# A hand-ordered attention and feed-forward kernel: a new order of all calls and loads, turns by DMA or TensorE chosen per tile, word-wide zero fills, and a tail in two unequal pieces

## The chip, the core and the metric

The kernel runs on one core of a Trainium2 chip. A core has five engines with queues of their own, which work side by side and wait for each other by semaphores: PE (TensorE, matrix products from SBUF into PSUM), DVE (VectorE), ACT (ScalarE), POOL (GpSimd) and SP (SyncE, which here only issues DMA transfers). Each engine takes its instructions strictly in the order of the program. The metric is the device time of one launch in microseconds (us).

## The reference

Two parts follow each other. The first is an attention over blocks whose keys and values are mixed across blocks by a matrix that is normalized in Sinkhorn's manner, five times over:

```python
P = sort_net                                   # [4, 8, 8, 8]
for _ in range(5):
    P = P - np.max(P, axis=-1, keepdims=True)
    P = np.exp(P)
    P = P / (np.sum(P, axis=-1, keepdims=True) + 1e-09)
    P = P / (np.sum(P, axis=-2, keepdims=True) + 1e-09)
k_sorted = np.einsum('bhij,bhjcd->bhicd', P, k_b)   # 8 blocks of 96 rows, head size 64
v_sorted = np.einsum('bhij,bhjcd->bhicd', P, v_b)
scores = scale * np.matmul(q_b, k_sb.transpose(0, 1, 2, 4, 3))
attn = softmax(scores)                         # within each block of 96
out = np.matmul(attn, v_sb)                    # [4, 8, 768, 64]
```

The second is a feed-forward part on the 3072 tokens of 512 features, with weights 512 x 2048 and 2048 x 512:

```python
h = x @ w_in
g = h * np.cos(h)
return (g @ w_out).astype(np.float32)          # [3072, 512]
```

## The kernel before

The 3072 tokens are worked in eight tiles of 384 (n = 0 to 7). A tile is half of one batch: four blocks of 96 rows (u = 0 to 3), all eight heads. The whole order of the program is one hand-written list of calls, PLAN; a loop (L722) takes the calls in turn and each emits its instructions. The list so fixes the order on every engine. A bank name in a call (B0, B1, B2: two PSUM banks each; C0, C1: one each) says where TensorE writes, and a call that starts with `e` empties that result with ACT (A) or DVE (V).

What a tile goes through, by call names:

- `qk` scores of one block: 4 matmuls of 192 columns (tile 0: 16 smaller ones). `mx` takes the maximum and subtracts it (DVE, L561 to L577), `ex` is the exponential (ACT, L582).
- The probabilities are turned, either by TensorE (`pp`, 8 transposes into PSUM, and an eviction) or by a DMA transpose issued by SP (`pd`, L592).
- `av` multiplies by the values (8 matmuls), `xn` divides by the sums (DVE, L619 and L621).
- The result is turned into xT, by TensorE (`xp`, 4 transposes and an eviction) or by DMA (`xd`, L630).
- `up` is the first projection, 4 accumulating matmuls per 128 of the 2048 hidden features (L653); `ga` takes the cosine by ACT (L663) and the product by DVE (L670) into `gall`; `dn` is the second projection, 4 matmuls of 512 columns a call, four calls for 128 rows (L678). `oc` copies out of PSUM, `st` stores.

Before the first tile there is the Sinkhorn normalization in two halves (`b_...` calls): short steps that go round ACT, PE and DVE. The mixed keys come from `k0`, `k1` and `kg`, the mixed values from `v0`, `v1` and `vg` (TensorE, then an eviction). Values for the upper positions are first reordered by POOL (`vp`, L487). The keys of a head pair lie in four slots: an eviction fills two of them, SP copies half of each to the other two (`ksw`, L472 and L474), and POOL writes zeros into what is left (`z_k`, L338), two of those fills after the copies have read their source.

Loads are issued by POOL (`ld_...`), because they convert float32 to bfloat16 on the way: q in two whole halves for tiles 0 and 1 (`ld_qr`, turned by TensorE with `q0` and `qp`), then by block (`ld_q`, turned by a DMA transpose, `qd`, L435); k and v for the first two batches (`ld_k`, `ld_v`) and for the other two (`ld_kg`, `ld_vg`); the weights in quarters (`ld_wi`, `ld_wo`). `hold` (L409) is a one-column copy on POOL that makes POOL wait for a given tile before it issues what follows.

`w` calls are idle matmuls on a constant tile (L343), 112 in all: they keep TensorE active where it would wait. The last 128 rows are not done by `dn` but by `tail` (L695): two halves of 256 columns, each with 16 matmuls, in the banks C0 and C1, emptied by ACT, and by DVE and ACT, and stored from SP and ACT.

## Time and profile before

| what | us |
|---|---|
| three runs | 242.86, 253.38, 252.88 |
| their median | 252.88 |
| span of the profiled execution | 242.1 |
| PE busy in it | 234.3 |
| DVE busy | 171.7 |
| ACT busy | 151.4 |
| POOL busy | 82.7 |
| bytes read from HBM, written | 27.27 MB, 6.29 MB |

The profile is of one execution with a span of 242.1 us, close to the lowest of the three runs. Busy time of PE contains the idle matmuls. The views quoted further down are the page of the profile, the windows (busy time of each engine and the granted TensorE clock in a stretch of time), the timeline of one engine (start, duration, instruction, and in brackets what ended its idle time), the chain (the work that ended last, followed back), and the view of one line of the program, which for a DMA gives the time from issue to landing.

### The profile page before, as it was taken

The page shows a single profiled execution, that of the slowest core. Times are in us where ns is not written, and L with a number is a line of the kernel's source. Part 1 is how long each engine was busy: PE and PEld are TensorE (multiplying, and loading weights), DVE is VectorE, ACT ScalarE, POOL GpSimd, SP SyncE. Part 2 cuts the span into 40 slices and gives each one's busy share as a digit, 9 for nine tenths or more (in the row PEclk, how much of TensorE's full clock was granted, in tenths as well). Part 3 has the DMA queues.
Part 4 walks back from the last instruction along what each step waited for, and adds up shares of the span by engine and source line. Part 5 has one row for each costly group of instructions (what it writes and reads, how often), then busy time and mean ns, then how long its engine had stood idle before and what let it go on. Part 6 is the DMA issues. An engine that isn't in the chain of part 4 may idle for free.

```text
span 242.1 us, 5306 instructions
## 1 busy us (share of the span) xinstructions
PE 234.3 (97%) x2166; PEld 152.0 (63%) x2166; DVE 171.7 (71%) x301; ACT 151.4 (63%) x210; POOL 82.7 (34%) x85
## 2 busy tenths in 40 slices
PE   8999999996999999999999999999999999999994
PEld 5867889954676566655666646655565555555553
DVE  5328767994688976898579989799969758616610
ACT  3175768675498777876587935683776479425601
POOL 8867599604981013999532300000000000000000
PEclk9999999997999999999999999999999999999999
DMA  7999996999999988798593974015862570450211
GB/s 88 212 203 195 205 190 79 125 226 154 139 152 216 191 160 171 114 145 116 94 130 73 102 124 105 0 27 115 212 102 49 129 81 2 109 190 0 87 71 62
DMA packets 64232, 29.91 MB, mean 124 GB/s; under 512 B 53584, under 2 KB 59728, under 8 KB 63952
## 3 DMA queue, kind: packets, MB, share of 16 engines
q0 software_dynamic: 26080, 13.63, 42.7%
q1 hardware_dynamic: 37616, 15.74, 29.9%
q8 instruction: 17, 0.28, 0.5%
q10 hardware_dynamic: 512, 0.20, 0.3%
q14 instruction: 7, 0.06, 0.1%
HBM read 27.27 MB, written 6.29 MB: 139 GB/s over the span
## 4 chain that ended last, share of the span: by engine, by line
PE 78%; DMA 10%; POOL 6%; ACT 2%; DVE 1%; issue 1%; DVEq 0%; ACTq 0%; SPq 0%
PE h L653 30%; PE o L678 25%; PE idle L343 7%; DMA pT<-p_buf 5%; DMA w_out_t<-in_moe_w_out_dram 5%; POOL vperm L487 3%; PE av L609 3%; PE sc L531 3%; PE vs L495 2%; PE o L701 1%; PE xps L638 1%; PE vs L513 1%; PE sk L354 1%; POOL q_mem L283 1%; PE pps L599 1%
## 5 line engine op out<-in xcount | busy, mean ns | idle before, releaser
L678 PE MATMUL o<-w_out_t,gall 128*128 128x512 bf16 x368 | 89.5, 382 | 1.9 <-DMA w_out_t<-in_moe_w_out_dram 1.9
L653 PE MATMUL h<-xT,w_in_t 128*128 128x384 bf16 (+1 forms) x576 | 88.6, 308 | 0.0
L670 DVE TENSOR_TENSOR gall<-c,h 128x768 bf16<-128x768 f32 x64 | 60.1, 950 | 22.4 <-ACT c L663 21.7
L663 ACT ACTIVATE c<-h,half_pi 128x768 f32<-128x768 f32 x64 | 57.2, 901 | 22.0 <-PE h L653 21.0
L653 PEld LDWEIGHTS <-w_in_t 128*128 128x128 bf16 x576 | 53.6, 98 | 27.1
L678 PEld LDWEIGHTS <-gall 128*128 128x128 bf16 x368 | 34.3, 99 | 33.8 <-issue 2.7
L582 ACT ACTIVATE p_buf<-s 96x768 bf16<-96x768 f32 x32 | 26.3, 839 | 4.5 <-DVE s L577 3.0
L487 POOL COPY vperm<-kv 128x1536 bf16<-128x1536 bf16 (+1 forms) x10 | 28.2, 2837 | 1.3 <-DMA kv<-in_v_dram 1.3
L568 DVE TENSOR_REDUCE mx<-sc 96x4 f32<-96x384 f32 (+1 forms) x39 | 28.1, 720 | 0.8 <-PE sc L531 0.7
L577 DVE TENSOR_TENSOR s<-sc,mx 96x384 f32<-96x384 f32 (+1 forms) x33 | 24.3, 736 | 2.2
L283 POOL DMA_DIRECT2D q_mem<-in_q_dram x24 | 18.8, 787 | 17.8 <-DMA q_turned<-q_mem 17.0
L621 DVE TENSOR_TENSOR xn<-av,r 96x512 bf16<-96x512 f32 x32 | 22.0, 687 | 1.1
L343 PE MATMUL idle<-warm 128*128 128x256 bf16 x112 | 18.6, 304 | 1.1 <-DVE half_pi L309 1.0
L247 ACT COPY o_s<-o 128x512 f32<-128x512 f32 (+2 forms) x10 | 5.3, 531 | 16.1 <-PE o L678 12.2
L343 PEld LDWEIGHTS <-warm 128*128 128x128 bf16 x112 | 11.2, 112 | 4.2 <-DVE half_pi L309 1.0
L338 POOL MEMSET kPg<- 64x768 bf16 (+1 forms) x8 | 13.6, 1704 | 0.2
L619 DVE RECIPROCAL r<-av 96x8 f32<-96x8 f32 x32 | 6.4, 199 | 9.2 <-PE av L609 9.1
L531 PEld LDWEIGHTS <-q_turned 128*128 128x128 bf16 x112 | 9.8, 99 | 4.3
L247 ACT COPY xT<-xps 128x384 bf16<-128x384 bf16 x11 | 5.3, 478 | 11.2 <-PE xps L638 11.2
L247 ACT COPY kv<-o 128x512 f32<-128x512 f32 x9 | 5.2, 580 | 10.6 <-PE o L678 10.6
L247 ACT CAST vS<-vs 96x512 bf16<-96x512 f32 x15 | 8.5, 585 | 5.0 <-PE vs L495 4.9
L531 PE MATMUL sc<-kPg,q_turned 128*128 128x192 bf16 x80 | 10.9, 246 | 0.0
(106 smaller groups left out, 229.9 us busy)
## 6 DMA issues: line engine op xcount, KB each, us to landing
out_dram<-kv SPq DMA_DIRECT2D x12, 256.0 KB, 2.4
out_dram<-o_s SPq DMA_DIRECT2D x11, 256.0 KB, 2.8
q_mem<-in_q_dram POOLq DMA_DIRECT2D x24, 96.0 KB, 4.7
w_out_t<-in_moe_w_out_dram POOLq DMA_DIRECT2D x4, 512.0 KB, 9.9
w_in_t<-in_moe_w_in_dram POOLq DMA_DIRECT2D x4, 512.0 KB, 18.5
kv<-in_v_dram POOLq DMA_DIRECT2D x2, 768.0 KB, 11.7
kv<-in_k_dram POOLq DMA_DIRECT2D x2, 768.0 KB, 8.5
kv<-in_v_dram POOLq DMA_DIRECT2D x6, 256.0 KB, 9.9
```

The costliest lines, as they stand in the source:

```text
L247: A.copy(dst, src)
L343: nc.tensor.matmul(idle[:], warm[:], warm[:, :1].to_broadcast([128, 256]), start=True, stop=True)
L487: G.tensor_copy(dst, src)
L531: nc.tensor.matmul(out, q_turned[n % 2][:, c:c + 128], keys, start=True, stop=True)
L568: V.reduce_max(m[:], scv, axis=AX.X)
L577: V.tensor_tensor(dst, scv, m.to_broadcast([blk, w, H2, blk]), op=ALU.subtract)
L582: A.activation(p[:, :, :blk], s_t.pop((n, u)).rearrange("p z a c -> p (z a) c"), AF.Exp, scale=scale)
L621: V.tensor_tensor(x[:], avv[:, :, :, :D], r.to_broadcast([blk, 2, H2, D]), op=ALU.mult)
L653: nc.tensor.matmul(hv[f], w_in_t[:, kk, (f0 + f) * 128:(f0 + f + 1) * 128], x_of(n)[:, kk, lo:hi], start=(kk == 0), stop=(kk == KC - 1))
L663: A.activation(cc, hh, AF.Sin, bias=half_pi[:, 0:1])
L670: V.tensor_tensor(dst, cc, hh, op=ALU.mult)
L678: nc.tensor.matmul(out_ps[n, ts][:], gall[:, g_at(n, f), ts * 128:(ts + 1) * 128], w_out_t[:, f, :], start=(f == 0), stop=(f == FC - 1))
```

## The change

All calls stand in a new order, with other banks and other evicting engines. Apart from that order:

- Idle matmuls: 36 instead of 112, and none at the end.
- Turns: tile 2's probabilities go by TensorE (12 `pp` and 20 `pd` calls instead of 8 and 24), and xT goes by DMA more often (18 `xd` and 14 `xp` instead of 12 and 20).
- Three of the four `hold` calls that made POOL wait for turned tiles go or move: `hold p 3 3` and `hold qt 1` go, `hold p 2 3` stands at the end of the list.
- Loads: sort_net first, then q, k, v, q, v, all of w_in, then w_out in the order 3, 0, 2, 1, then the second batch's keys. Before, the first quarter of w_out stood ahead of v and w_in, and the other three behind the second batch's keys.
- `z_k` writes its zeros as 32-bit words. The copy that makes `maskp` is a call of its own.
- `ex` takes a free buffer from a list that `pd` and `pp` fill again.
- `dn` accumulates its four parts in any order; the call that comes first opens the accumulation and the fourth closes it.
- The last tile's results go to memory of their own in the key buffer (`kept` 2). The last 128 rows are done by `dl`, in 384 and 128 columns, in two banks, interleaved with the other rows of the tile; `ol` empties and stores them (DVE and SP, ACT and ACT).

The first and last lines of the new list, and the diff of the functions:

```diff
+    "ld_s", "z_warm", "w 3 B2", "z_id", "z_mask", "w 3 B2", "z_maskp", "b_max 0", "b_max 1", "ld_qr 0",
+    "b_exp0 0", "b_ci 0", "b_exp0 1", "ld_k 0", "b_rows 0", "w 1 C1", "b_turn 0 C0", "b_cols 0", "w 2 B2",
+    "b_ci 0", "w 2 B0", "b_exp 0", "z_same", "b_sum 0 B1", "ld_v 0", "q0 1 B0", "z_tail", "b_inv 0",
+    "b_norm 0", "w 4 C0", "ld_qr 1", "b_ci 1", "b_ci 0", "b_exp 0", "z_pi", "z_k 0 1", "b_sum 0 C0",
+    "z_pad", "ld_v 1", "e q0 1 V", "b_inv 0", "b_norm 0", "q0 3 B2", "b_ci 0", "q0 2 B0", "b_rows 1",
+    "b_exp 0", "q0 0 C0", "b_sum 0 C1", "b_inv 0", "w 1 B1", "e q0 0 A", "z_ones 0", "b_norm 0", "w 3 C0",
+    "ld_wi 2", "ld_wi 3", "b_ci 0", "z_order", "e q0 2 V", "w 1 C0", "b_exp 0", "ld_wi 1", "b_sum 0 C0",
+    "b_inv 0", "b_norm 0", "b_ci 0", "b_turn 1 C1", "w 2 C0", "w 4 C0", "ld_wi 0", "b_end 0", "e q0 3 A",
+    "b_cols 1", "k0 0 0 16 C0", "k0 0 16 16 B2", "k0 0 32 16 B0", "b_ci 1", "e k0 0 0 16 V",
+    "e k0 0 16 16 V", "b_v B1", "k0 1 16 16 C0", "k0 1 32 16 C1", "e k0 0 32 16 A", "e k0 1 32 16 A",
+    "e b_v V", "qk 0 3 2 B0", "v0 2 24 8 B1", "b_exp 1", "e k0 1 16 16 V", "qk 0 0 2 B2", "ld_wo 3",
+    "e v0 2 24 8 A", "v0 2 8 8 C1", "vp 0 32 16", "k0 1 0 16 B1", "e v0 2 8 8 A", "mx 0 3 2",
+    "e k0 1 0 16 A", "ksw 0 1", "v0 2 16 8 B0", "v0 2 32 8 C1", "qk 0 1 2 B1", "w 1 C0", "e v0 2 32 8 A",
+    "w 2 C0", "vp 0 48 16", "b_sum 1 C0", "mx 0 0 2", "e v0 2 16 8 A", "w 1 B2", "ex 0 0 0", "mx 0 1 2",
...
+    "ga 6 12 2 0 384", "up 6 10 2 0 384 B2", "pd 7 0", "av 7 1 B1", "st 4 2 S", "dn 6 0 0 C1", "st 5 2 S",
+    "ex 7 3 1", "pd 7 3", "dn 6 2 1 B0", "st 5 1 S", "hold p 2 3", "xn 7 1", "av 7 0 B1", "st 2 2 S",
+    "xn 7 0", "dn 6 1 3 C0", "ga 6 10 2 0 384", "dn 6 2 0", "dn 6 1 1", "av 7 3 B1", "xd 7 1", "xd 7 0",
+    "xn 7 3", "dn 6 1 0", "xd 7 3", "av 7 2 B2", "dn 6 2 2", "dn 6 0 2", "dn 6 1 2", "xn 7 2", "dn 6 0 1",
+    "xd 7 2", "dn 6 2 3", "oc 6 2 A 1", "up 7 6 2 0 384 B2", "up 7 4 2 0 384 B0", "up 7 10 2 0 384 B1",
+    "oc 6 1 V 1", "ga 7 6 2 0 384", "dn 6 0 3", "ga 7 4 2 0 384", "up 7 2 2 0 384 B2", "dn 7 1 1 C0",
+    "st 6 1 S", "ga 7 10 2 0 384", "up 7 12 2 0 384 B0", "up 7 0 2 0 384 B1", "oc 6 0 A 1", "st 6 0 S",
+    "ga 7 2 2 0 384", "ga 7 12 2 0 384", "up 7 8 2 0 384 B2", "up 7 14 2 0 384 B0", "ga 7 0 2 0 384",
+    "dn 7 0 0 B1", "dn 7 0 1", "dl 0 1 C1", "st 6 2 S", "ga 7 8 2 0 384", "ga 7 14 2 0 384", "dn 7 1 3",
+    "dl 0 2", "dn 7 0 3", "dn 7 1 2", "st 5 0 S", "dn 7 1 0", "oc 7 1 A 2", "dl 0 3", "dn 7 0 2",
+    "oc 7 0 A 2", "dl 0 0", "dl 1 2 B2", "dl 1 3", "dl 1 0", "dl 1 1", "st 7 1 S", "st 7 0 S", "ol 0 V S",
+    "ol 1 A A",
...
@@ -327,6 +328,8 @@
 
     def z_same():
         V.tensor_copy(same, rows_of)
+
+    def z_maskp():
         V.tensor_copy(maskp.rearrange("p (b e x) -> p b e x", b=2, e=2),
                       maskh.rearrange("p (b x e) -> p b e x", b=2, e=2))
 
@@ -335,7 +338,7 @@
     def z_k(g, part):
         t, (rows, s) = KP[g], ((slice(64, 128), 1), (slice(0, 64), 2),
                                (slice(64, 128), 0), (slice(0, 64), 3))[part]
-        G.memset(t[rows, s], 0.0)
+        G.memset(t[rows, s].rearrange("p m t -> p (m t)").bitcast(FP32), 0.0)
 
     def w(times, pool):
         idle = pool[0].tile([128, 256], FP32, name="idle", tag=pool[1])
@@ -518,7 +521,7 @@
 
     ROWS = 2
     s_t, pb, pT, av_t, xn_t, xT, sc_t = {}, {}, {}, {}, {}, {}, {}
-    cnt = [0]
+    free = list(range(NP))
 
     def scores(n, u, h2, out):
         g, b2, ih = where(n)
@@ -577,8 +580,8 @@
             V.tensor_tensor(dst, scv, m.to_broadcast([blk, w, H2, blk]), op=ALU.subtract)
 
     def ex(n, u, late):
-        p = p_bufs[cnt[0] % NP]
-        cnt[0] += 1
+        i = free.pop(0)
+        p = p_bufs[i]
         A.activation(p[:, :, :blk], s_t.pop((n, u)).rearrange("p z a c -> p (z a) c"),
                      AF.Exp, scale=scale)
         if late:
@@ -586,14 +589,18 @@
             t = vperm[:, z * w:(z + 1) * w].rearrange("p (a c) -> p a c", c=blk)
         else:
             t = ptp.tile([128, H, blk], BF16, name="pT", tag="pT")
-        pT[n, u], pb[n, u] = t, p
+        pT[n, u], pb[n, u] = t, i
 
     def pd(n, u):
+        i = pb.pop((n, u))
+        free.append(i)
         nc.sync.dma_start_transpose(
-            out=pT[n, u][:], in_=pb.pop((n, u)).rearrange("p a c -> p (a c)"))
+            out=pT[n, u][:], in_=p_bufs[i].rearrange("p a c -> p (a c)"))
 
     def pp(n, u, pool):
-        p = pb.pop((n, u))
+        i = pb.pop((n, u))
+        free.append(i)
+        p = p_bufs[i]
         ps = pool[0].tile([128, H, 128], BF16, name="pps", tag=pool[1])
         for a in range(H):
             nc.tensor.transpose(ps[:blk, a, :blk], p[:, a, :blk], ident[:blk, :blk])
@@ -602,7 +609,7 @@
     def av(n, u, pool):
         g, b2, ih = where(n)
         a = pool[0].tile([128, 2, 512], FP32, name="av", tag=pool[1])
-        pt = pT.pop((n, u)).rearrange("p a c -> p (a c)")
+        pt = pT[n, u].rearrange("p a c -> p (a c)")
         for e in range(H):
             h2, hp = e // 2, e % 2
             w = 128 if e < H - 1 else blk
@@ -669,56 +676,57 @@
             hh = hh.rearrange("p z (f c) -> p z f c", f=half)
         V.tensor_tensor(dst, cc, hh, op=ALU.mult)
 
-    out_ps, o_sb = {}, {}
-
-    def dn(n, ts, part, pool=None):
-        if part == 0:
-            out_ps[n, ts] = pool[0].tile([128, Dm], FP32, name="o", tag=pool[1])
-        for f in range(part * FC // 4, (part + 1) * FC // 4):
-            nc.tensor.matmul(
-                out_ps[n, ts][:], gall[:, g_at(n, f), ts * 128:(ts + 1) * 128], w_out_t[:, f, :],
-                start=(f == 0), stop=(f == FC - 1))
+    out_ps, o_sb, parts = {}, {}, {}
+
+    LAST = (B * S // TC - 1, TC // 128 - 1)
+    CUT = (slice(0, 3 * Dm // 4), slice(3 * Dm // 4, Dm))
+
+    def dn(n, ts, part, pool=None, z=None):
+        c = slice(0, Dm) if z is None else CUT[z]
+        key = (n, ts, z)
+        if key not in out_ps:
+            out_ps[key] = pool[0].tile([128, c.stop - c.start], FP32, name="o", tag=pool[1])
+            parts[key] = 0
+        parts[key] += 1
+        fs = range(part * FC // 4, (part + 1) * FC // 4)
+        for f in fs:
+            nc.tensor.matmul(
+                out_ps[key][:], gall[:, g_at(n, f), ts * 128:(ts + 1) * 128], w_out_t[:, f, c],
+                start=(parts[key] == 1 and f == fs[0]), stop=(parts[key] == 4 and f == fs[-1]))
 
     def oc(n, ts, eng, kept):
         if kept:
-            z = (n % 2 * 3 + ts) * 2 * Dm
-            o_s = vbuf[:, z:z + 2 * Dm].bitcast(FP32)
+            z = (ts if kept == 2 else n % 2 * 3 + ts) * 2 * Dm
+            o_s = (vbuf, vbuf, kbuf[:, CD // 2:])[kept][:, z:z + 2 * Dm].bitcast(FP32)
         else:
             o_s = op.tile([128, Dm], FP32, name="o_s", tag="o_s")[:]
-        copy_on(eng, o_s, out_ps.pop((n, ts))[:])
+        copy_on(eng, o_s, out_ps.pop((n, ts, None))[:])
         o_sb[n, ts] = o_s
 
     def st(n, ts, queue):
         r0 = n * TC + ts * 128
         queue.dma_start(out=out[r0:r0 + 128, :], in_=o_sb.pop((n, ts)))
 
-    def tail():
-        n, ts, w = 7, TC // 128 - 1, Dm // 2
-        for z in range(2):
-            pool = POOL[("C0", "C1")[z]]
-            o = pool[0].tile([128, w], FP32, name="o", tag=pool[1])
-            for f in range(FC):
-                nc.tensor.matmul(
-                    o[:], gall[:, g_at(n, f), ts * 128:(ts + 1) * 128],
-                    w_out_t[:, f, z * w:(z + 1) * w], start=(f == 0), stop=(f == FC - 1))
-            o_s = op.tile([128, w], FP32, name="o_s", tag="o_s")
-            for e, (eng, dma) in enumerate(
-                    (((A, nc.scalar),), ((V, nc.sync), (A, nc.scalar)))[z]):
-                c = slice(e * w // 2, (e + 1) * w // 2) if z else slice(0, w)
-                copy_on(eng, o_s[:, c], o[:, c])
-                dma.dma_start(
-                    out=out[n * TC + ts * 128:(n + 1) * TC, z * w:(z + 1) * w][:, c],
-                    in_=o_s[:, c])
+    def dl(z, part, pool=None):
+        dn(*LAST, part, pool, z)
+
+    def ol(z, eng, queue):
+        c = CUT[z]
+        r0 = LAST[0] * TC + LAST[1] * 128
+        at = CD // 2 + LAST[1] * 2 * Dm
+        o_s = kbuf[:, at:at + 2 * Dm].bitcast(FP32)[:, c]
+        copy_on(eng, o_s, out_ps.pop((*LAST, z))[:])
+        queue.dma_start(out=out[r0:r0 + 128, c], in_=o_s)
 
     calls = dict(
         ld_s=ld_s, ld_k=ld_k, ld_v=ld_v, ld_kg=ld_kg, ld_vg=ld_vg, ld_qr=ld_qr, ld_q=ld_q,
         ld_wi=ld_wi, ld_wo=ld_wo, z_id=z_id, z_p=z_p, z_ones=z_ones, z_warm=z_warm, z_pi=z_pi,
-        z_pad=z_pad, z_tail=z_tail, z_order=z_order, z_mask=z_mask, z_same=z_same, z_k=z_k, w=w,
+        z_pad=z_pad, z_tail=z_tail, z_order=z_order, z_mask=z_mask, z_same=z_same, z_maskp=z_maskp, z_k=z_k, w=w,
         b_exp0=b_exp0, b_rows=b_rows, b_turn=b_turn, b_cols=b_cols, b_exp=b_exp, b_sum=b_sum,
         b_norm=b_norm, b_inv=b_inv, b_ci=b_ci, b_max=b_max,
         b_end=b_end, b_v=b_v, hold=hold, q0=q0, qp=qp, qd=qd, k0=k0, k1=k1, kg=kg,
         ksw=ksw, vp=vp, v0=v0, v1=v1, vg=vg, qk=qk, mx=mx, ex=ex, pd=pd, pp=pp, av=av, xn=xn, xd=xd,
-        xp=xp, up=up, ga=ga, dn=dn, oc=oc, st=st, tail=tail)
+        xp=xp, up=up, ga=ga, dn=dn, oc=oc, st=st, dl=dl, ol=ol)
     made = {}
     for call in PLAN:
         name, *args = call.split()
@@ -728,7 +736,7 @@
             continue
         key = (name, *(a for a in args if a not in POOL))
         args = [POOL[a] if a in POOL else a for a in args]
-        if name == "st":
+        if name in ("st", "ol"):
             args[2] = QUEUE[args[2]]
         args = [ENG[a] if isinstance(a, str) and a in ENG else a for a in args]
         args = [int(a) if isinstance(a, str) and a.isdigit() else a for a in args]
```

211 rows, old and new, of the table PLAN are left out of this document.

## The prediction

> **What bounds the kernel now.** First the page's busy shares and its chain, and the group of the idle matmuls among the costliest groups.
>
> ```profile
> span 242.1 us, 5306 instructions
> PE 234.3 (97%) x2166; PEld 152.0 (63%) x2166; DVE 171.7 (71%) x301; ACT 151.4 (63%) x210; POOL 82.7 (34%) x85
> ...
> PE 78%; DMA 10%; POOL 6%; ACT 2%; DVE 1%; issue 1%; DVEq 0%; ACTq 0%; SPq 0%
> ...
> L343 PE MATMUL idle<-warm 128*128 128x256 bf16 x112 | 18.6, 304 | 1.1 <-DVE half_pi L309 1.0
> ```
>
> TensorE is the engine of the end: 97% busy, 78% of the chain. But 112 of its 2166 matmuls compute nothing (the program calls them `w`), so busy is not useful here. The second view is the windows, cut where the work changes: Sinkhorn, tile 0's attention, tile 0's up-projections, the place around a wait, and the rest.
>
> ```profile
> core 0: us, PE busy (x) PEld busy (x) DVE busy (x) ACT busy (x) POOL busy (x), PEclk, DMA share, GB/s
> ...
> 14.90:33.80 18.90, 18.47 (x346) 15.29 (x346) 12.44 (x22) 11.27 (x21) 14.75 (x10) 1.00 1.22 204
> 33.80:53.60 19.80, 19.80 (x277) 17.02 (x274) 16.24 (x27) 15.64 (x22) 12.18 (x12) 1.00 1.01 145
> 53.60:61.40 7.80, 5.91 (x46) 3.56 (x43) 3.89 (x10) 4.71 (x8) 3.65 (x4) 0.78 0.99 173
> ...
> 67.50:120.00 52.50, 52.03 (x447) 32.35 (x446) 42.28 (x72) 39.56 (x54) 28.60 (x25) 1.00 0.99 154
> 120.00:170.00 50.00, 49.80 (x383) 29.84 (x381) 43.51 (x67) 33.10 (x41) 6.48 (x10) 1.00 0.55 83
> 170.00:234.00 64.00, 64.00 (x418) 35.74 (x417) 42.09 (x57) 37.23 (x45) 0.00 (x0) 1.00 0.39 90
> ```
>
> From 67.5 to 234 us TensorE pauses 0.47 + 0.20 us in all. No new order can win there; it can only lose. What can be won is the time before the first up-projection, one disturbed place, and the end. TensorE's timeline shows the three.
>
> ```profile
> 1.01 4.88 PE L343 MATMUL idle<-warm 128*128 128x256 bf16 x22 [1.01 <-DVE half_pi L309]
> ...
> 14.87 1.36 PE L446 MATMUL ks<-bd,kv 64*128 64x32 bf16 x48
> ...
> 33.78 1.49 PE L653 MATMUL h<-xT,w_in_t 128*128 128x192 bf16 x16
> ...
> 53.56 1.03 PE L678 MATMUL o<-w_out_t,gall 128*128 128x512 bf16 x4
> 56.48 1.02 PE L678 MATMUL o<-w_out_t,gall 128*128 128x512 bf16 x4 [1.89 <-DMA w_out_t<-in_moe_w_out_dram]
> 57.34 0.28 PE L354 MATMUL sk<-E,kPg 128*128 128x8 f32 x2
> 57.48 1.47 PE L678 MATMUL o<-w_out_t,gall 128*128 128x512 bf16 x4
> ...
> 233.99 1.16 PE L343 MATMUL idle<-warm 128*128 128x256 bf16 x9
> ```
>
> The first up-projection starts at 33.78 us. From there every microsecond of TensorE's stream is useful except the wait before 56.48, its after-effect, and nine idle matmuls at 233.99. So I make the sum as a shift of TensorE's stream: how much earlier or later the same work ends.
>
> **The change part by part.**
>
> *Weights of the down-projection.* The wait at 56.48 ends with the landing of the last quarter of w_out:
>
> ```profile
> 44.77 11.67 DMA w_out_t<-in_moe_w_out_dram
> ```
>
> The matmuls at 53.56 should last 4 x 0.216 = 0.86 us, to 54.42; the next ones start at 56.48, which is 2.06 us lost. After it four matmuls take 1.47 instead of 1.03 us, and the window around it has a clock of 0.78: 0.22 x 7.8 = 1.7 us more. In the new order all four quarters are queued on POOL before the second batch's keys, and the down-projection takes the quarters in the order of the loads (3, 0, 2, 1). Ahead of the last quarter stand two 384 KB halves of q, three 768 KB loads of k and v, and 4 + 4 weight quarters of 512 KB: 7.3 MB. At the 204 GB/s of the second window that is 36 us, so about 38 us. TensorE asks for that quarter after 32.7 us of useful work, which by the old pace is 49 us or later. The wait goes: **-3.7 us**. Late next would be the second batch's keys, 0.8 MB or 4 us behind (42 us), first used near 53 us.
>
> *Nine idle matmuls before the tail.* They lasted 234.99 - 233.99: **-1.0 us**. The two pieces of the last row block (384 and 128 columns) now go to banks of their own, so nothing has to be emptied first, and their 32 matmuls stream the same columns. What lies behind the last matmul I leave at its old length, within 0.3 us: the last piece is smaller, but the 384-column store is larger than any that was last before.
>
> *Turns on TensorE instead of by DMA.* Tile 2's four probability turns (32 transposes) come to TensorE, and six fewer xT turns stay there.
>
> ```profile
> 61.95 0.36 PE pps L599 x8
> ...
> 63.65 0.17 PE xps L638 x4
> ```
>
> 4 x 0.36 - 6 x 0.17 = **+0.4 us** of TensorE work. The four evictions that come with it lie in a stretch where the vector engine is busy 42.3 of 52.5 us. The removed DMA turns take some of the 0.67 us of later pauses with them: **-0.4 us**.
>
> *The way to the first up-projection.* Three things change: the zero fills leave the start, 36 idle matmuls stand where 112 stood, and more useful work is pulled ahead of the first up-projection: both q turns of tile 1 (2 x 0.46 us), eight v1 matmuls, two score parts, one xT turn and two Sinkhorn sums, together 2.0 us at the pitches of the same calls in TensorE's timeline. What sets the moment is not TensorE but the vector engine behind the scores:
>
> ```profile
> 13.84 0.35 DVE L392 SCALAR_TENSOR_TENSOR bd<-maskp,ci,T 128x128 bf16<-128x128 f32 x1
> ...
> 18.37 0.95 DVE L561 TENSOR_REDUCE mx<-sc 96x8 f32<-96x768 f32 x1 [3.92 <-PE sc L542]
> 19.36 0.95 DVE L562 TENSOR_TENSOR s<-sc,mx 96x768 f32<-96x768 f32 x1
> ...
> 26.51 0.55 DVE L249 COPY pT<-pps 96x768 bf16<-96x768 bf16 x1
> ...
> 29.60 0.19 DVE L619 RECIPROCAL r<-av 96x8 f32<-96x8 f32 x1
> 29.83 0.69 DVE L621 TENSOR_TENSOR xn<-av,r 96x512 bf16<-96x512 f32 x1
> ```
>
> Its queue in the new order, from the first maximum on: four `mx` at 1.97 us (7.9), one Sinkhorn step of the other half (0.6), three evictions of 0.55 (1.65), four `xn` at 0.84 (3.4): 13.5 us, and 0.6 us more through the last turn on TensorE. When does it start? Before, 18.37. The three key evictions now go to both engines, which saves up to 0.8 us: 17.6 at best. Against it stands the clock: TensorE no longer spins before the keys, and the 22 first matmuls above took 222 ns each where the nine at the end took 111, so a TensorE that comes from rest runs at half speed. Five key blocks and one score block (1.36 / 3 + 0.47 us and the like, 2.7 us together) would then take 2.7 us longer: 20.3 at worst. I take the middle, 18.9, and so 18.9 + 13.5 + 0.6 = 33.0 us for the first up-projection (31.7 to 34.4). That is 0.8 us earlier, with 2.0 us more already done: **-2.8 us** (-4.1 to -1.4). The Sinkhorn chain itself I leave at 13.84: it loses a 1.4 us zero fill that ran beside its first copies and gains a fill and two evictions between its steps.
>
> Behind that point the stream may still be at half clock for some microseconds, since TensorE waits for the vector engine now and then without a filler. None of it costs nothing, and one after-effect as at 57 us costs 1.7: I take 0.7, **+0.7 us**. The Trainium skill ("TensorE: Matmul & The Clock Gate", Part 1) says that the clock is halved by default, comes up after a window of some 3.4 us of activity, and falls back only after an idle window of that length. The first half agrees with the 4.88 us row; the second does not quite, since here 2.06 us of idling was followed by half speed. By the page's rule no gap of the new order would be long enough, the 0.7 us would be zero and the sum 0.7 us less.
>
> *Zeros as words, and copies of keys beside them.* A zero fill of 64x1536 on POOL costs this:
>
> ```profile
> 60.41 1.37 POOL L338 MEMSET kP<- 64x1536 bf16 x1
> 63.26 2.68 POOL L338 MEMSET kPg<- 64x3072 bf16 x1
> ```
>
> Twice the elements, twice the time, so half the elements should be half (0.7 and 1.35 us); if bytes counted it would stay. The fills matter where they now stand between the last key copy and the first score. Copies by SP (L472, L474) and the q turn behind them (L435, the last row) land as the views of these three lines say, in this order:
>
> ```profile
> L472 SPq DMA_DIRECT2D kPg<-kPg x2: 472/480/489, 37.1 to 100.9; - x2
> ...
> DMA to landing us min/median/max: 2.1/3.9/6.5
> ...
> L474 SPq DMA_DIRECT2D kPg<-kPg x2: 586/587/588, 37.7 to 101.4; - x2
> ...
> DMA to landing us min/median/max: 2.1/5.8/7.0
> ...
> DMA to landing us min/median/max: 3.5/4.1/7.0
> ```
>
> For tiles 2 and 3 the last k1 block is now only 6.5 us of TensorE work ahead of the first score of tile 2. Eviction 0.9, two issues 1.1, landing 2.1 to 7.0, two fills 1.4: 5.5 to 10.4 us, so a wait of 0 to 4 us. The queues should be quiet then, because POOL stands at the fill and issues no load: I take 0.4. For tiles 4 and 5 the second copy stands 4.8 us of work ahead of the first score, and SP is free for it some 1.7 us sooner, 6.5 us; issue 1.1, landing 2.1 to 5.8, two fills 2.7: 5.9 to 9.6, so 0 to 3.1 us, and 0.4 again. **+0.8 us** (0 to 7). Two of the four holds go and a third stands at the end of the list, so loads start earlier beside DMA turns; tile 3's four turns are at 14, 7, 7 and 10 us from score to use, about as before, and I add nothing.
>
> **The sum.** -3.7 - 1.0 + 0.4 - 0.4 - 2.8 + 0.7 + 0.8 = -6.0 us. The profiled execution has a span of 242.1 us; the lowest of the three runs, 242.86, is that with 0.8 us around it. 242.9 - 6.0 = **236.9 us**. The median of the three runs, 252.88, stands 10 us above both; nothing in the profile shows what those 10 us are, so the forecast is for an execution like the profiled one.
>
> **The rivals.**
>
> *Half clock through the start (slower).* One mechanism: with 36 idle matmuls TensorE is never active long enough before the first up-projection. Of the 18.9 us of the second window 40 idle matmuls and the pauses beside them took 6.7 by TensorE's timeline; with the 2.0 pulled ahead, and 0.3 for a Sinkhorn product that now stands before the keys, 13.9 us of useful work lie between the keys (14.9) and that point. At half clock they take 27.8, TensorE and not the vector engine sets the moment, and it is 42.7 instead of 33.0: +9.7. The first two up-projections at half speed add 2.6: 249.2 us. For it speaks the row of 22; against it, that a TensorE that is the bound is busy, and a busy one came up to speed within the 4.88 us of that row. It decides from about 6 us lost, which makes the kernel as slow as before.
>
> *The copies and fills become the wait.* If the landings are the upper ones (7.0 and 5.8 us) the two places cost 4 and 3 us instead of 0.8, one of them with a 1.7 us after-effect: 236.9 + 7.9 = 244.8; with only one of them, 241. The same holds, smaller, if a fill costs by bytes.
>
> *The loads stay late.* The order of the loads is new, but the sum of bytes is not; if w_out's last quarter still comes 2 us after TensorE asks, the 3.7 us are not won: 240.6 us. Against it stand 11 us of margin by the sum above.
>
> **How the numbers follow.** About 2%, 4.9 us, is what a measurement of this kernel can tell from no change: faster means under 238.0, slower over 247.7. Forecast with its own range of 232.5 to 239: 0.56, of which 0.05 lies above 238.0. Copies and fills: 0.18, all within 2%. Late loads: 0.11, within 2%. Half clock: 0.15, of which 0.13 is over 247.7. So faster 0.51, same 0.36, slower 0.13. The low end of the range is the forecast with the best start (-4.1 for -2.8), no half clock and no new wait: 236.9 - 1.3 - 0.7 - 0.8 = 234.1, and 1.6 us for a Sinkhorn chain that starts earlier without its zero fill: 232.5. The high end takes in both fills at their worst and the mild half of the half-clock case: 246.
>
> **What would show it.** Right: no TensorE wait for w_out, a clock of 1.00 around 57 us, the first up-projection at 32 to 34 us, no idle matmuls at the end, a fill of 64x768 words in 0.7 us. Wrong: first up-projections in 2.6 instead of 1.3 us; a TensorE wait of over 1 us before the first scores of tile 2 or tile 4; a wait for w_out or for the second batch's keys near 50 us; a pause between 67 us and the end that sums to over 2 us.

## The result and the profile after

The change made the kernel slower. Four runs of the new kernel took 255.34, 256.78, 259.23 and 259.40 us, four of the old one beside them 242.86, 243.92, 252.88 and 253.38. Part of the executions of either kernel are several us longer than the others, those of the old one at a lower granted clock, so the ratio, here and below, is taken over the shorter ones alone: **1.051 [1.042, 1.061]**. The forecast was 236.9 us with a range of 232.5 to 246. The profiled execution took 255.34 us, with a span of 253.5 us against 242.1.

The first view of the new profile is the windows of TensorE, cut as those of before. The columns are the same: length, busy time of the engines, granted clock, share of the DMA engines.

```profile
core 0: us, PE busy (x) PEld busy (x) DVE busy (x) ACT busy (x) POOL busy (x), PEclk, DMA share, GB/s
...
14.90:38.80 23.90, 22.70 (x371) 19.77 (x372) 16.67 (x37) 13.80 (x25) 20.34 (x17) 1.00 1.21 211
38.80:67.50 28.70, 28.64 (x364) 22.57 (x362) 24.75 (x52) 19.60 (x26) 5.19 (x6) 1.00 0.53 79
67.50:100.00 32.50, 27.41 (x231) 16.95 (x228) 23.19 (x38) 16.82 (x22) 18.78 (x23) 0.89 1.16 173
100.00:140.00 40.00, 35.88 (x300) 22.39 (x298) 27.24 (x44) 26.10 (x33) 17.53 (x15) 1.00 0.79 110
140.00:234.00 94.00, 93.06 (x650) 52.72 (x649) 74.59 (x107) 56.88 (x68) 3.45 (x6) 1.00 0.49 91
```

The stage that held the wait for w_out is clean: 28.64 us of 28.70. But the stretch from 67.5 to 140 us, in which TensorE had paused at most 0.7 us before, now has 9.2 us of pauses (5.09 + 4.12). The timeline of TensorE says what ended them (start, duration, and in brackets the idle time and its end):

```profile
71.01 0.34 PE L534 MATMUL sc<-kP,q_turned 128*128 128x192 bf16 x2 [0.59 <-DMA q_turned<-q_mem]
...
93.98 0.50 PE L534 MATMUL sc<-kP,q_turned 128*128 128x192 bf16 x2 [4.50 <-DMA q_turned<-q_mem]
94.28 1.91 PE L693 MATMUL o<-w_out_t,gall 128*128 128x512 bf16 x4
...
128.86 0.43 PE L616 MATMUL av<-vS,pT 96*128 96x65 bf16 x8 [1.20 <-DMA pT<-p_buf]
129.13 1.03 PE L693 MATMUL o<-w_out_t,gall 128*128 128x512 bf16 x4
...
134.35 4.06 PE L660 MATMUL h<-xT,w_in_t 128*128 128x384 bf16 x24 [1.71 <-DMA xT<-xn]
```

Every one of the four pauses waits for a transfer that SP issues: tile 2's q turn, tile 3's q turn, a probability turn, an xT turn. Behind the largest pause the four matmuls at 94.28 take 1.91 us, where four of the same kind take 1.03 elsewhere (the row at 129.13 us): half clock, which the trace records from 91.73 for 6.83 us.

To add this up I sum the lengths that TensorE's useful calls have at full speed, and call what is left of the time lost. The table is worked out from the timelines of both kernels.

| up to | lost before, us | lost after, us | difference |
|---|---|---|---|
| first up-projection (33.8 / 38.8 us) | 18.8 | 22.0 | +3.2 |
| tile 0's down-projection (63 to 66 us) | 22.8 | 22.5 | -0.3 |
| about 99 us | 23.3 | 30.2 | +6.9 |
| 140 us | 23.7 | 35.2 | +11.5 |
| last matmul | 25.4 | 37.1 | +11.7 |

So the gain at w_out (3.5 us: 4.0 us were lost in that stage before, 0.5 after) paid for the start, and all of the loss arises between 67 and 140 us: 7.2 us up to and behind tile 3's q turn, 4.6 us around tile 3's other turns. Both places lie where the prediction said that no new order could win, only lose.

The start is the second reading. The clock column says 1.00 from the beginning, but the lengths of the same instructions say otherwise. Before, the view by tile has for the idle matmuls and for tile 0's probability turns (count, then minimum, median and maximum in ns):

```profile
L343 PE MATMUL idle<-warm x112: 269/273/421, 1.0 to 234.9; 128*128 128x256 bf16 x112
...
L599 PE MATMUL pps<-ident,p_buf x32: 208/208/243, 25.9 to 30.5; 96*96 96x96 bf16 x32
```

and after:

```profile
L346 PE MATMUL idle<-warm x36: 272/417/422, 1.0 to 63.1; 128*128 128x256 bf16 x36
...
L606 PE MATMUL pps<-ident,p_buf x32: 280/280/316, 30.3 to 34.9; 96*96 96x96 bf16 x32
```

The median moves from the fast to the slow length. The trace's first recorded change of the clock, to full, is at 37.11 us after and at 6.72 us before; the column shows 1.00 only because it has no record earlier. TensorE ran its whole start at half speed, and the vector engine waited for it:

```profile
20.17 0.95 DVE L564 TENSOR_REDUCE mx<-sc 96x8 f32<-96x768 f32 x1 [0.32 <-PE sc L545]
...
32.00 1.20 DVE L250 COPY q_turned<-qps 128x768 bf16<-128x768 bf16 x2 [0.23 <-PE qps L431]
...
37.59 0.69 DVE L628 TENSOR_TENSOR xn<-av,r 96x512 bf16<-96x512 f32 x1
```

From the first maximum at 20.17 to the end of the last `xn` at 38.28 are 18.1 us, of which about 4 are waits for TensorE.

The third reading is POOL. Its timeline, with one row of ACT's:

```profile
43.66 0.33 POOL L301 MEMSET p_buf<- 96x256 bf16 x1
67.50 0.73 POOL L341 MEMSET kP<- 64x768 f32 x1 [23.51 <-DMA kP<-kP]
...
72.82 1.55 POOL L284 DMA_DIRECT2D q_mem<-in_q_dram  x2
...
89.33 1.37 POOL L341 MEMSET kPg<- 64x1536 f32 x1 [4.19 <-DVE kPg L250]
...
90.74 0.58 ACT L248 CAST kPg<-ks 128x512 bf16<-128x512 f32 x1 [3.02 <-POOL kPg L341]
```

POOL stands for 23.5 us at the first fill of kP1 that follows a copy (`z_k 1 3`), with nothing to do. Behind it in its queue are the loads of the second batch's keys and values and tile 3's q, which it issues between 69 and 83 us. The last quarter of that q landed at 82.75 us, and the chain of waits shows the turn that needs it:

```profile
82.91 11.03 DMA q_turned<-q_mem
```

The zero fills did become half as long, as forecast: 0.73 us for 64x768 words, 1.37 us for 64x1536, where 1.37 and 2.68 us stood.

### The profile page after: what moved, and what is told of

Read it like the earlier page. It is cut to its first block, busy times and chain, and to the rows that moved or that the text cites. A ratio compares the mean times of both kernels' runs of the same rounds, so it can differ in the third digit from the quotient of the medians.

```text
span 253.5 us, 5171 instructions
## 1 busy us (share of the span) xinstructions
PE 235.1 (93%) x2098; PEld 150.9 (60%) x2098; DVE 178.3 (70%) x315; ACT 144.4 (57%) x193; POOL 73.7 (29%) x83
## 4 chain that ended last, share of the span: by engine, by line
PE 76%; DMA 11%; ACT 6%; issue 2%; SPq 1%; POOL 1%; DVE 1%; ACTq 0%
PE h L660 31%; PE o L693 24%; DMA q_turned<-q_mem 6%; PE sc L534 3%; PE av L616 3%; PE idle L346 3%; DMA out_dram<-o_s 2%; PE pps L606 2%; PE vs L498 2%; ACT pair L248 2%; DMA vperm<-p_buf 2%; PE sk L357 1%; ACT p_buf L585 1%; DMA xT<-xn 1%; PE sc L545 1%
## 5 line engine op out<-in xcount | busy, mean ns | idle before, releaser
L693 PE MATMUL o<-w_out_t,gall 128*128 128x512 bf16 (+2 forms) x400 | 94.8, 375 | 0.0
L660 PE MATMUL h<-xT,w_in_t 128*128 128x384 bf16 (+1 forms) x576 | 87.2, 308 | 2.5 <-DMA xT<-xn 1.7
L693 PEld LDWEIGHTS <-gall 128*128 128x128 bf16 x400 | 36.7, 100 | 31.5 <-issue 1.1
L580 DVE TENSOR_TENSOR s<-sc,mx 96x384 f32<-96x384 f32 (+1 forms) x33 | 24.3, 736 | 2.2
L248 ACT COPY kv<-o 128x512 f32<-128x512 f32 (+1 forms) x10 | 5.5, 549 | 20.6 <-PE o L693 20.6
L534 PEld LDWEIGHTS <-q_turned 128*128 128x128 bf16 x112 | 9.9, 99 | 11.4 <-DMA q_turned<-q_mem 5.6
L341 POOL MEMSET kPg<- 64x384 f32 (+1 forms) x8 | 7.2, 900 | 20.0 <-ACT pair L248 13.2
L248 ACT CAST kPg<-ks 128x512 bf16<-128x512 f32 x11 | 6.4, 578 | 11.1 <-PE ks L449 4.6
L616 PEld LDWEIGHTS <-pT 96*128 96x128 bf16 (+1 forms) x160 | 8.4, 113 | 4.4 <-DMA pT<-p_buf 2.9
L346 PE MATMUL idle<-warm 128*128 128x256 bf16 x36 | 9.7, 388 | 1.4 <-DVE warm L307 1.0
L248 ACT CAST vS<-vs 96x512 bf16<-96x512 f32 x13 | 7.4, 586 | 4.7 <-PE vs L498 3.6
## 6 DMA issues: line engine op xcount, KB each, us to landing
out_dram<-kv SPq DMA_DIRECT2D x14, 256.0 KB, 2.3
out_dram<-o_s SPq DMA_DIRECT2D x9, 256.0 KB, 3.7
```

The source lines that it names most:

```text
L248: A.copy(dst, src)
L534: nc.tensor.matmul(out, q_turned[n % 2][:, c:c + 128], keys, start=True, stop=True)
L580: V.tensor_tensor(dst, scv, m.to_broadcast([blk, w, H2, blk]), op=ALU.subtract)
L660: nc.tensor.matmul(hv[f], w_in_t[:, kk, (f0 + f) * 128:(f0 + f + 1) * 128], x_of(n)[:, kk, lo:hi], start=(kk == 0), stop=(kk == KC - 1))
L693: nc.tensor.matmul(out_ps[key][:], gall[:, g_at(n, f), ts * 128:(ts + 1) * 128], w_out_t[:, f, c], start=(parts[key] == 1 and f == fs[0]), ...
```

## The experiments

Twelve kernels were run. The table has the time of the profiled execution, all runs, and the ratio to the kernel before in runs on the same chip; the text below names each in words.

| kernel | profiled, us | all runs, us | ratio [95%] |
|---|---|---|---|
| after | 255.34 | 255.3 to 259.4 | 1.051 [1.042, 1.061] |
| after, v loads held back | 262.05 | 257.5 to 262.1 | 1.060 [1.051, 1.068] |
| after, key copies early | 255.85 | 253.2 to 255.9 | 1.044 [1.036, 1.051] |
| after, more idle matmuls at the start | 259.92 | 259.2 to 259.9 | 1.063 [1.058, 1.068] |
| before, w_out early | 243.13 | 243.1 to 249.5 | 0.998 [0.990, 1.006] |
| after, q loads early | 265.05 | 256.0 to 265.1 | 1.056 [1.047, 1.065] |
| after, idle matmuls between small ones | 258.06 | 255.3 to 261.2 | 1.056 [1.047, 1.065] |
| before, a third of the idle matmuls | 246.27 | 246.3 to 249.9 | 1.021 [1.012, 1.031] |
| after, three mends | 256.15 | 248.9 to 256.8 | 1.031 [1.017, 1.046] |
| after, loads and fills early | 253.73 | 251.7 to 255.4 | 1.042 [1.035, 1.050] |
| after, all mends | 242.70 | 242.7 to 245.2 | 1.002 [0.997, 1.008] |
| after, all mends but the start | 244.89 | 244.7 to 246.0 | 1.011 [1.005, 1.018] |
| before with the parts that pay | 242.71 | 239.5 to 248.2 | 0.990 [0.984, 0.997] |

### What delays tile 3's q turn

First, the values' loads beside the turn were held back until it had landed.

```
-"ld_vg 4 6", "ld_vg 0 6",
...
-"qd 3",
+"qd 3", "hold qt 1", "ld_vg 4 6", "ld_vg 0 6", "ld_vg 5 6", "ld_vg 3 6", "ld_vg 1 6", "ld_vg 2 6",
```

> The changed kernel with its six loads of the later values (0.25 MB each) issued only after the q turn of tile 3 has landed. Theory (the turn stands in the DMA queues behind those loads): the turn, which took 11.0 us from issue to landing, lands in 3.5 to 5 us, TensorE's 4.7 us wait for it before the first score of tile 3 goes, and with it some 2 us of half clock behind it: 5 to 7 us off the changed kernel's 253.5 us span. Rival (the wait comes from the late load of q itself): the load still lands near 82.7 us and the turn near 88 or later, under 3 us are won, or new waits for the later values take the gain.

The turn itself became quick, 3.52 us from issue to landing instead of 11.03. But it could be issued only at 85.19 us, since its q had landed at 85.0, as the rival said, and TensorE's wait grew to 5.32 us. It was ended by something else, a fill on POOL, an eviction on ACT behind it, and TensorE behind that:

```profile
88.76 0.19 POOL L408 CAST held<-q_turned 128x1 f32<-128x1 bf16 x1 [12.04 <-DMA q_turned<-q_mem]
...
95.22 1.37 POOL L337 MEMSET kPg<- 64x1536 f32 x1 [0.78 <-DVE kPg L246]
...
96.63 0.59 ACT L244 CAST kPg<-ks 128x512 bf16<-128x512 f32 x1 [6.45 <-POOL kPg L337]
...
97.27 0.48 PE L530 MATMUL sc<-kP,q_turned 128*128 128x192 bf16 x2 [5.32 <-ACT kPg L244]
```

My hold had put a wait in front of the two fills of the second batch's keys, and an ACT eviction waits for those, and TensorE for its bank. So the run shows two things, the slow turn beside loads and a second cause behind the first, and as a test of the time it spoiled itself.

Next, only tile 3's q loads were taken out from behind POOL's wait.

```
+"ld_q 3 1", "ld_q 3 3", "ld_q 3 0", "ld_q 3 2",
 "z_p 2",
...
 "z_k 1 3",
...
-"ld_q 3 1",
...
-"ld_q 3 2",
```

> The new order with one thing moved: the four loads of tile 3's q stand ahead of POOL's fill of tile 2's keys instead of behind it, so POOL issues them at about 44 us and not at 71 to 74. Theory: POOL's 23.5 us wait at that fill holds the loads back, the late load makes tile 3's q turn land at 93.9 us, and the turn is what TensorE waits for at 89 us. Then the turn lands before 88 us, the 4.7 us wait and the half clock behind it (2.1 us) go, and the profiled time falls from 255.3 to about 249 (248 to 251). Rival: the turn is slow because of the traffic around it (second batch of keys and values on the same DMA engines); then it still takes about 10 us, the wait stays over 3 us and the time over 253.

The loads landed at 50.6 us, 32 us earlier, and nothing was won: the shortest execution took 256.0 us. The turn was now issued at 69.24 us, straight after tile 2's, and 0.3 us before the first load of the second batch's keys. In the profiled execution (9 us longer than the shortest) both stood still: the turn took 20.4 us, and the load of 768 KB

```profile
69.53 20.34 DMA pair<-in_k_dram
...
89.92 0.61 PE L462 MATMUL ks<-bd,pair 128*128 128x128 bf16 x4 [9.52 <-DMA pair<-in_k_dram]
```

held TensorE for 9.5 us at the first `kg` block. What the two took in the shorter executions is not recorded. The early q alone is not the cure; whether the turn has to be clear of the large loads as well is what the next runs try.

The run with three mends moved the key loads too, with the other two mends told below. At this place it adds to the edit of the run before:

```
 "ld_q 3 2",
+"ld_kg 0 2", "ld_kg 1 2",
 "z_p 2",
...
-"ld_kg 0 2",
...
-"ld_kg 1 2",
```

> The new order with the suspects mended together: tile 3's q loads and the second batch's key loads ahead of POOL's fill, the copies for tiles 4 and 5's keys straight behind their last key block, and the idle matmuls of the start raised as in the run that tests the start alone. If the three losses are separate and add up: 6.8 us for the wait at 89 us and its half clock, 4 us for the start, 3 us for the turns around 130 us, so about 255.3 - 13 = 242 (240 to 245). Rival: what is won at one place is given back at the next (a later turn meets later loads); then the time stays over 247.

The shortest execution, 248.9 us, is far above the 242 asked for and in the range of the rival. The profiled one, 256.15 us, ran at half clock from 24.4 to 41.4 us. In it the turn landed at 76.6 us, 3.7 us after its issue. The wait of 4.5 us fell to 1.9 us, and this rest is the second cause, seen in the clear:

```profile
94.60 0.59 ACT L245 CAST kPg<-ks 128x512 bf16<-128x512 f32 x1 [3.02 <-POOL kPg L338]
...
95.24 0.33 PE L531 MATMUL sc<-kP,q_turned 128*128 128x192 bf16 x2 [1.90 <-ACT kPg L245]
```

The change put the fills `z_k 2 1` and `z_k 2 0` between two evictions into the same tile (before, one lay ahead of all evictions and the other behind the last): eviction, fill, eviction go one after the other, and the score waits for the last. In the new kernel the same 3.02 us of ACT's wait were hidden under the late turn. The next run has the loads early and moves the fills ahead of all `kg` blocks as well; it is the new order otherwise:

```
 "ld_kg 1 2", "z_p 2",
+"z_k 2 1", "z_k 2 0",
...
-"z_k 2 1",
...
 "e kg 0 4 V",
-"z_k 2 0",
...
 "e kg 44 4 A",
```

> The new order with only POOL's order mended around 45 to 75 us: tile 3's q loads and the second batch's key loads ahead of the fill at which POOL stands, and the two fills of the second batch's keys behind them, ahead of all key copies (in the new order they stand between two copies, and the run with several mends showed an ACT copy waiting 3.0 us for one of them while tile 3's q turn had already landed). Theory: the wait at 89 us has two causes, one behind the other, a late q turn and fills between the copies; with both gone the wait (4.7 us) and its half clock (about 2 us) go entirely, and the time is 255.3 - 6.5 = 249 (247.5 to 250.5) at undisturbed clock. Rival: a third cause stands behind them (the vector engine's queue, or the q turn is slow again), and over 2 us of the wait stay; then 251 to 254.

The wait at 89 us vanished, and its half clock with it: no pause over 0.4 us between 78 and 122 us. But only 2 to 4 us reached the end, and the time (251.7 to 255.4 us) is the rival's. The two q turns now follow each other on SP, the first landed 6.2 us after its issue instead of 4.4, and tile 2's first score waits:

```profile
66.86 3.69 SPq L434 DMA_TRANSPOSE q_turned<-q_mem  x2
...
73.09 0.34 PE L530 MATMUL sc<-kP,q_turned 128*128 128x192 bf16 x2 [2.40 <-DMA q_turned<-q_mem]
```

with half clock for 3.41 us after it. Further on the waits at tile 3's other turns grew, to 1.46 us for a probability turn and 3.06 us for an xT turn, where the new kernel has 1.20 and 1.71. Both causes were right, and most of the gain went into a third wait and into these turns.

### The copies for tile 4's keys

```
 "e kg 24 4 A",
+"ksw 2 0", "ksw 2 1",
...
 "z_ones 1",
-"ksw 2 0",
 "vg 36 4 B0",
-"ksw 2 1",
```

> The changed kernel with the two key copies of tiles 4 and 5 issued by SP as soon as the keys are there, ahead of the turns of tile 3 and not between its third and fourth. Theory (the two copies and the store just ahead of it delay the fourth probability turn, and by SP's order everything behind it): that turn lands in 2.8 to 3.5 us instead of 5.7, TensorE's waits between 125 and 137 us shrink from 5.4 to under 2 us, 3 to 4.5 us off the span. Rival (the xT turns by DMA are what comes late): the wait of 1.9 us for the xT turn before the second up-projection of tile 3 stays, and 1 to 2 us are won.

The fourth turn landed 3.84 us after its issue instead of 5.73, and the pauses and slow stretches between 122 and 137 us shrank from 5.0 to about 1.6 us. At tile 4's xT turns a new one stood, followed by 3.41 us of half clock. One of these turns took 4.50 us to land, where the two took 2.3 and 2.4 in the new kernel; POOL now issued three of tile 7's q loads from 1.4 us behind it on. That these loads are the cause was not tested.

```profile
130.76 4.06 PE L656 MATMUL h<-xT,w_in_t 128*128 128x384 bf16 x24 [0.17 <-DMA xT<-xn]
...
158.37 12.24 PE L656 MATMUL h<-xT,w_in_t 128*128 128x384 bf16 x64 [2.15 <-DMA xT<-xn]
```

The lost time at the end was that of the new kernel, 37.2 us, and the ratio, 1.044, lies in the interval of the new kernel's.

### The start

First the idle matmuls at the places where the new order has them were raised from 36 to 92:

```
-"w 3 B2",
+"w 10 B2",
...
-"w 2 C0", "w 4 C0",
+"w 8 C0", "w 8 C0",
```

> The changed kernel with 56 more idle matmuls in its start (before and between the Sinkhorn steps, and ten more up to tile 0's turns). Theory (TensorE runs at half clock from the first instruction to about 37 us, since it is never active long enough): the idle matmuls come down from 213 to 111 ns before the keys, a score block takes 0.47 and a turn block 0.36 us instead of 0.78, and the first up-projection comes at 33 to 35 us instead of 38.8: 4 to 6 us off the span. Rival (the start is set by the Sinkhorn chain, which starts with a table load that now waits for the data, and by the order of the evictions): the first up-projection stays at 37 to 39 us, and the idle matmuls only fill the waits.

The clock came up at 5.8 us, the first keys at 15.7 instead of 16.8 us, and then it fell again:

```profile
15.70:19.50 3.80, 3.80 (x125) 3.70 (x124) 3.13 (x5) 1.71 (x4) 3.80 (x3) 1.00 0.92 188
19.50:39.50 20.00, 19.46 (x252) 16.65 (x252) 12.69 (x24) 12.59 (x22) 18.75 (x17) 0.50 1.23 210
```

TensorE was busy without a pause in the 3.8 us before the fall, with small matmuls only. The first up-projection came at 39.5 us. All four executions took 259.2 to 259.9 us and recorded a mean clock of 0.947 to 0.954, so the fall was not an accident of one of them. So long idle matmuls were put between the small ones, as in the kernel before (106 in all), and the table preload back to the front.

```
 "ld_s", "z_warm",
+"z_pi",
...
 "k0 0 32 16 B0",
+"w 6 C1",
...
+"w 6 B1",
 "v0 2 24 8 B1",
...
+"w 5 C1",
 "v0 2 8 8 C1",
```

> The new order with its idle matmuls raised from 36 to 106, put as long pieces between the small matmuls from the first key block to tile 0's probability turns as well as before them, and the table preload back at the front. Theory: the late first up-projection (38.8 us against 33.8) comes from a TensorE that is left at half clock, and only long matmuls in between hold the clock; then the granted clock is up by about 7 us and stays up, k0 starts near 15 us, the first up-projection at 34 to 35 us, and the time falls by about 4 us, from 255.3 to 251. Rival: the extra useful work ahead of the first up-projection and the vector engine's queue set that moment; then it stays at 37 us or later whatever the clock, and the time within 2 us of the new order.

The clock stayed up from 5.39 us on; the keys started at 14.2 us and the first up-projection at 36.7 us, 2.1 us earlier, short of the 34 to 35 that the theory asked for and near the rival's 37. The time did not follow: the gain was lost at 130 us, where an xT turn was waited for 4.1 us. And the vector engine still waited:

```profile
25.09 0.95 DVE L561 TENSOR_REDUCE mx<-sc 96x8 f32<-96x768 f32 x1 [2.78 <-PE sc L542]
```

because the new order puts key and value blocks between the second and third scores of tile 0. How much of that wait is the order and how much my idle matmuls was not separated.

The other direction settles the clock itself: the kernel before, with 31 idle matmuls for 103 ahead of the first up-projection and nothing else changed.

> The kernel before with its idle matmuls ahead of the first up-projection cut to about a third (103 to 31), nothing else changed: this part of the change alone. Theory: TensorE stays at half clock through the start, the first up-projection comes 3 to 5 us later (37 to 39 us instead of 33.8), and the time rises from 243 to 246 to 248. Rival: the vector engine sets that moment and the idle matmuls only fill pauses; then it stays within 1 us of 33.8 and the time is that of the kernel before.

```profile
L649 PE MATMUL h<-xT,w_in_t x16: 246/367/368, 37.7 to 39.8; 128*128 128x192 bf16 x16
```

The first up-projection moved from 33.8 to 37.7 us and started at half speed (367 ns for 246), and the clock was recorded as full only from 39.5 us. Time: 1.021 [1.012, 1.031]. This part of the change alone costs about 5 us (2.8 to 7.4 by the interval). In the profiled execution, the shortest, 2.3 us of it are left in the span (244.4 against 242.1): TensorE asks later for w_out, and the wait for it is gone.

### w_out

The order before, with w_out's last three quarters directly behind the first `vp 2 16 16`:

```
 "vp 2 16 16",
+"ld_wo 1", "ld_wo 2", "ld_wo 3",
...
-"ld_wo 1",
...
-"ld_wo 2",
...
-"ld_wo 3",
```

> The kernel before with only the last three quarters of w_out issued earlier on POOL, straight behind the second batch's keys, the last quarter of w_in and one reordering copy (some 35 us instead of 41 to 45). If the wait at 56.5 us is a matter of the load order alone, it goes, with its half clock: 3.7 us off 242.1. If the bytes ahead set the landing, half of it stays, or another load is late in its place (values or q blocks), and under 2 us are won.

The wait for w_out and the half clock were gone, and a 2.47 us wait came in at 47 us, for a fill of tile 1's keys. SP issued the two key copies ahead of that fill at 37.42 and 37.96 us, nearly as before (37.12 and 37.66). But beside the three loads of 512 KB they took 8.0 and 8.1 us to land, not 2.1, and POOL stood idle at the fill until then:

```profile
45.54 1.52 POOL L336 MEMSET kPg<- 64x768 bf16 x2 [1.97 <-DMA kPg<-kPg]
...
47.11 0.32 PE L529 MATMUL sc<-kPg,q_turned 128*128 128x192 bf16 x2 [2.47 <-POOL kPg L336]
```

So another transfer was late in its place, as the second half of the expectation allows, and no change in time is shown (0.998).

### All mends together

The last runs put all of it into the new order: loads and fills as above, tile 2's q turn at 48 us with the key loads held until it has landed, tile 4's q turn and tile 6's q loads ahead of tile 3's turns, the copies early, the idle matmuls of the start, and tile 7's last xT turn on TensorE.

```
+"ld_q 3 2", "qd 2", "hold qt 0", "ld_kg 0 2", "ld_kg 1 2", "z_p 2", "z_k 2 1", "z_k 2 0",
...
 "st 1 0 S",
+"qd 4",
...
 "ld_q 5 1",
+"ld_q 5 2", "ld_q 6 1", "ld_q 6 3", "ld_q 6 0", "ld_q 6 2",
...
-"xd 7 2",
...
+"xp 7 2 B1", "e xp 7 2 V",
```

> The new order with every loss mended that the runs have named: the loads and fills as in the run beside it, tile 2's q turn issued at about 50 us and the second batch's key loads held until it has landed, longer idle matmuls in the start, the key copies of tiles 4 and 5 early, tile 4's q turn and tile 6's q loads ahead of tile 3's turns, and the last tile's last xT turn on TensorE. If the losses are separate: the best run of the earlier mix, 248.9, less 2.9 for the fills, 0.9 for tile 2's q turn, 2.6 at tile 3's xT turns and 1 at the last tile: 241.5 (239 to 245), level with the kernel before. Rival: losses move on to the next transfer; then it stays at 246 or more.

The same once more with the start of the new order:

> The run with every loss mended, but with the start of the new order again (36 idle matmuls, the table preload late); all the later repairs stay. Theory: the start's loss is separate from the later ones and is carried to the end; first up-projection at 38 to 39 us instead of 36.4, and the time 2 to 3 us over the mended run's 242.7 to 245.2: 245 to 247.5. Rival: later waits take the shift in, since transfers keep their own times; then less than 1 us of it arrives at the end, 243 to 245.

The mended order took 242.7 us in its profiled execution, level with the kernel before: 1.002 [0.997, 1.008]. Its windows from the first up-projection on are nearly free of pauses:

```profile
36.40:67.50 31.10, 31.04 (x385) 24.09 (x384) 26.07 (x55) 20.45 (x27) 15.24 (x20) 1.00 1.20 180
67.50:100.00 32.50, 32.42 (x280) 20.77 (x279) 29.21 (x49) 23.22 (x30) 18.45 (x19) 1.00 0.91 125
100.00:140.00 40.00, 39.18 (x320) 24.06 (x319) 32.11 (x47) 28.90 (x36) 10.06 (x9) 1.00 0.56 97
```

The lost time at the end is 24.3 us where the new kernel has 37.1. Without the start's part (the idle matmuls and the place of the table preload together) the first up-projection comes 2.4 us later (38.8 for 36.4), the lost time at the end is 26.5 us, and the run takes 2.2 us more (244.89 for 242.70): with the later waits mended, the loss at the start is carried to the end nearly in full. So of the 12.6 us between the profiled executions of the new kernel and its mended form about 2.2 are the start, and 10.4 the order of loads, fills, copies and turns.

What the runs credit to the change was then put into the order before: word fills, the tail in own banks and memory without the idle matmuls, and w_out's quarters on the places of q loads so that POOL issues as many loads before each fill as it did.

```
-"ld_q 2 1",
+"ld_wo 1",
...
-"ld_q 2 2", "ld_wo 1",
+"ld_wo 2", "ld_wo 3",
...
-"ld_wo 2",
+"ld_q 2 1",
...
-"ld_wo 3",
+"ld_q 2 2",
...
-"w 9 B0",
+"dl 0 0 B0",
...
-"tail",
+"dl 1 0 B1", "dl 1 1", "dl 1 2", "dl 1 3", "ol 0 V S", "ol 1 A A",
```

> The order of before with only those parts of the change that the runs credit: word fills, the tail in banks and memory of its own without the nine idle matmuls, and w_out's last quarters loaded ahead of two of tile 2's q loads (places swapped, so that POOL issues as many loads before each fill as before). Expected: 1.0 us for the idle matmuls, 2 to 3.7 us for the wait for w_out and the half clock behind it: 242.9 - 3.5 = 239.4 (238.5 to 241). Rival: the later q loads delay tile 2's q turn and its first score waits instead; then only the 1.0 us is won, 242.

This beats both kernels, the one before by about 1%: 0.990 [0.984, 0.997], with 239.45 and 240.40 us as its lowest runs. The profiled one, 242.71, had half clock from 27.6 to 37.8 us. No wait for w_out is left; 0.90 us at a fill of tile 1's keys took its place. POOL again stood at that fill until the key copies had landed, 6.9 and 7.1 us after their issue beside three loads of w_out:

```profile
46.94 0.41 POOL L339 MEMSET kPg<- 64x384 f32 x1 [7.19 <-DMA kPg<-kPg]
...
48.02 0.33 PE L532 MATMUL sc<-kPg,q_turned 128*128 128x192 bf16 x2 [0.90 <-POOL kPg L339]
```

## Why the prediction was wrong

**w_out (-3.7): right.** The last quarter landed at 42.21 us (38 forecast), the second batch's keys for tile 1 at 46.76 (42), and TensorE waited for neither. Of the 4.0 us that this stage lost before 0.5 were left: 3.5 us were won.

**Idle matmuls before the tail (-1.0): right.** After the last matmul 3.0 us follow, against 3.4 before.

**The way to the first up-projection (-2.8): the sign was wrong.** The forecast was 33.0 us, the range up to 34.4, measured 38.8. Two steps failed. The first maximum was put at 18.9, the middle between the clock being up and down, and came at 20.17, the end for a half clock (20.3). And the 13.5 us of vector work were added up as if it never waited: the work was about that, but some 4 us of waits for a TensorE at half speed lay between. The kernel with a third of the idle matmuls shows that their removal alone does this (33.8 to 37.7 us). The rival of the half clock was right in its mechanism and far off in its price: lost time rose by 3.2 us, not by 9.7, because much of the slow work lay under the vector engine, and because the clock was up again when the long matmuls began.

**After-effects (+0.7): at the wrong place.** None behind the first up-projection; 2.1 us came behind the wait at 89 us.

**Fills and copies (+0.8): this step carries most of the error.** It said: "The queues should be quiet then, because POOL stands at the fill and issues no load". That POOL would stand was seen. What was not asked is what is queued behind it: the loads of tile 3's q and of the second batch. The first score of tile 2 waited 0.6 us, near the 0.4 taken; tile 3's score, which the new order asks for more than 5 us of work earlier, lost 6.9 us with its half clock. At the second place the forecast was again 0.4 us (bounds 0 to 3.1), and the score itself waited 0.35; the loss of 5.0 us came to the turns behind the copies on SP. The step priced the transfer that it looked at and not the ones behind it.

**Tile 3's four turns ("about as before, and I add nothing"): wrong.** The fourth turn is issued right behind the two copies and lands 5.73 us later, the q and xT turns stand behind it on SP, and TensorE waits 1.20 us for that turn and 1.71 us for an xT turn.

**The rivals.** *Loads stay late* named the mechanism for w_out, where it did not hold; it held for loads that it did not name. *Copies and fills become the wait* (244.8) named the right places, but by its own mechanism it would have been right only for the 0.6 and the 0.35 us. *Half clock* came nearest in time (249.2) by luck, since most of the loss arose elsewhere. The argument against it, that a busy TensorE came up to speed within the row of 4.88 us, misread that row: its 22 matmuls follow each other at 213 ns, and full clock is recorded from 6.72 us, after its end.

In sum, forecast against measured in the stages of the table: start with after-effects -2.1 and +3.2, w_out -3.7 and -3.5, the q turns 0.4 and 7.2, tile 3's other turns 0.4 and 4.6, the rest up to the last matmul -1.4 and +0.2 (the idle matmuls are gone, but a wait of 0.9 us for a probability turn at 203 us has come), the amount of useful work and what follows it 0.4 and -0.3. The differences are 5.3, 0.2, 6.8, 4.2, 1.6 and -0.7: together the 17.4 us between -6.0 and +11.4.

What stays open: how much of the start's 3.2 us is the later place of two scores; how much of its mend is the table preload; and why a turn beside loads takes 11 us in one run and 20 in another. The mends of the last runs were not each tried alone.

## What to carry to other kernels

When an instruction that waits is moved ahead on an in-order engine, list everything queued behind it, DMA issues first, and ask when each of them is now issued and what it then meets; the wait itself may cost nothing. A wait that is mended can hide a second one of nearly the same length, and time won at one place is spent at the next transfer that keeps its own time. A load that is issued earlier also slows the copies that it now runs beside. So mend and measure several places together before judging one. Idle matmuls that look like waste may hold the clock: judge it by the lengths of equal instructions, not by the clock column alone.
